# Attention, MoE and FFN in one kernel: GpSimd's weight chunk placed between the scatters of a pair's two tiles, for four pairs

## The chip, the cores and the metric

The kernel runs on one core of a Trainium2 chip. The metric is the device time of one execution in microseconds (us), as the median of several runs. Engines: PE (TensorE), DVE (VectorE), ACT (ScalarE), GpSimd (POOL in the profile) and SyncE (SP), which issues most transfers.

## What is computed

Three layers follow one another on 2304 tokens (4 sequences of 576) of 512 values:

```python
scores = scale * q @ k.T ; bias = slope[h] * -|i - j| ; mask = (0 <= i - j < 128)
x   = softmax(where(mask, scores + bias, -1e9)) @ v            # 8 heads of 64
...
noisy = x @ w_gate + log1p(exp(x @ w_noise)) * noise           # 8 experts, top 2 of each token
x   = sum over the two experts e: weight * (relu(x @ w1[e]) @ w2[e])
...
out = (relu(x @ w_in) ** 2) @ w_out                            # 512 -> 2048 -> 512
```

## The kernel before

Tokens are taken in 18 tiles of 128 rows. The attention stage is one loop over `v` from -2 to 38 (L553): an even `v` is the first four heads of tile `v // 2`, an odd one the other four. A turn of the loop issues three products of three neighbouring steps: the scores of step `v + 2` (`s_step`, matmuls at L257), the transposes of the probabilities of step `v + 1` (`t_step`, L279) and probabilities times values of step `v` (`pv_step`, L303). The score matmuls are small, 64 rows by 64 to 192 columns, so PE runs through many instructions in a microsecond here. Later stages use matmuls of 256 to 512 columns.

Tiles are gated in pairs: pair `p` is tiles `2p` and `2p + 1`, nine pairs from 0 to 8. What a pair needs is hung into the loop by a table written out by hand (L514 to L545, `at(v, slot, step)`): two transposed copies (`gate_t`, L333, L337), the gate product (`gate_w`, L344), the noise part (`gate_m`, L352), top 2 and ranks on DVE (`gate_o`, `rank`, `place`). `place` ends with `pos` (L422), which says for both tiles of the pair to which slot each token goes. Then `scatter(i)` (L425) writes the token numbers of tile `i` into the table `slots` in DRAM, for the first and the second expert of each token: two indirect transfers of 128 numbers, issued by GpSimd, each behind a `memset` of one element called `spacer` (L427, L428). For pair `p` the first tile's scatters are hung at turn `4p + 7`, the second's at turn `4p + 8`, but `pos` for both exists at the first; GpSimd works in order, and finds all four ready one behind the other.

Three times (`early_table`, L500, behind pairs 2, 4 and 6) a part of `slots` is read back and GpSimd gathers a tile of rows for the first expert (`gather`, L438), which PE transposes at L448.

Beside this the loop prepares the first seven of 64 weight chunks. A chunk is 128x1024 numbers; `prep_one` (L97) has GpSimd write a rounded copy (cast, L108) and the remainder (subtract, L110). The raw chunk is loaded by SyncE into one of two buffers (`load_to`, L88); `prep_one(i)` makes sure that chunk `i` is loaded and, when done, asks for chunk `i + 1`. The loop calls it at turns 2, 10, 14, 18, 22, 26 and 30 (L573); as GpSimd is ahead of the loop's code there, a chunk stands directly behind the four scatters of the pair before.

Of the kernel before, what the change touches and what calls it, by code (L numbers as in the profile page):

```python
# [49 lines left out]
def attn_moe_ffn(ctx: ExitStack, tc: tile.TileContext, qt, kt, vt, wgn, noise, w1, w2, w_in, w_out,  # L50
# [35 lines left out]
    nload, nprep = [0], [0]  # L86

    def load_to(n):  # L88
        while nload[0] < min(n, len(srcs)):
            i = nload[0]  # L90
            src, a = srcs[i]
            r = rawp.tile([128, 1024], F32, name="raw", tag="raw", bufs=2)
            nc.sync.dma_start(out=r if a is None else r.rearrange("p (a d) -> p a d", a=a), in_=src)
            raws[i] = r
            nload[0] += 1

    def prep_one(hi="act", lo="dve"):  # L97
        i = nprep[0]
        nprep[0] += 1
        load_to(i + 1)  # L100
        r = raws.pop(i)
        g, m = (i // 4) % 3, (i % 4) * 2048
        t = big["wb" if g else "wa"] if g < 2 else late["wc"]
        c = [t[:, m:m + 1024], big["wt"] if g == 1 and m == 6144 else t[:, m + 1024:m + 2048]]
        if hi == "act":
            nc.scalar.activation(out=c[0], in_=r, func=AF.Copy)
        else:
            nc.gpsimd.tensor_copy(c[0], r)  # L108
        eng = nc.vector if lo == "dve" else nc.gpsimd
        eng.tensor_tensor(out=c[1], in0=r, in1=c[0].bitcast(F32), op=OP.subtract)  # L110
        chunks[i] = c
        load_to(i + 2)


    width = {"wb": 7168, "wt": 1024, "xa": 3072, "wa": 8192, "ha": 6144, "xb": 3072, "hb": 4096, "tt": 1152, "wc": 8192, "ex": 3584, "et": 512}
# [36 lines left out]
    def load_q(i):  # L152
        Q[i] = qp.tile([128, 4, 128], F32, name="q", tag="q", bufs=4)
        nc.sync.dma_start(out=Q[i], in_=qt[i])

    def load_k(b, k0=0, k1=S):
        if b:
            K[b] = qp.tile([128, 4, S], F32, name="k", tag="k", bufs=2)
        nc.sync.dma_start(out=K[b][:, :, k0:k1], in_=kt[b][:, :, k0:k1])

    def load_v(n):
        b, p = divmod(n, 5)
        V[n] = qp.tile([128, 2, 8, 65], F32, name="v", tag="v", bufs=5)
        nc.sync.dma_start(out=V[n], in_=vt[b][:, 2 * p:2 * p + 2])
# [62 lines left out]
    def run(v, slot):  # L227
        for f, a in todo.pop((v, slot), []):
            f(*a)
# [42 lines left out]
    def t_step(v):  # L272
        PT[v] = []
        for j, p2 in enumerate(P2.pop(v)):
            flat = p2.rearrange("p a n -> p (a n)")
            ps = bank("a")[:, :384]
            for m in range(3):
                sl = slice(m * 128, (m + 1) * 128)
                nc.tensor.transpose(ps[:, sl], flat[:, sl], ident)  # L279
            pt = wk.tile([128, 3, 128], F32, name="pt", tag="pt", bufs=4)  # L280
            nc.scalar.activation(out=pt, in_=ps.rearrange("p (m c) -> p m c", m=3), func=AF.Copy)
            PT[v].append(pt)

    def pv_step(v):
        i, g = divmod(v, 2)
        px = bank("b")[:, :, :130].rearrange("p a (j d) -> p a j d", j=2)
        PX[i, g] = px
        mms = []
        for part in range(2):
            for j, pt in enumerate(PT[v]):  # L290
                for x in range(2):
                    b, t = divmod(2 * i + x, TB)
                    sl = slice(64 * x, 64 * x + 64)
                    for a in range(2):
                        h = 4 * g + 2 * j + a
                        if part == 0:
                            if a or t:
                                mms.append((x, a, j, pt[:, 2 * a, sl], vs(b, t - 1 + a)[:, h, :]))
                        elif a == 0 or t > 1:
                            r = slice(64 * a, 64 * a + 64)  # L300
                            mms.append((x, a, j, pt[r, 1, sl], vs(b, t - 2 if a else t + 1)[r, h, :]))
        for n, (x, a, j, l, r) in enumerate(mms):
            nc.tensor.matmul(px[64 * x:64 * x + 64, a, j, :], l, r,  # L303
                             start=not any(m[:2] == (x, a) for m in mms[:n]),
                             stop=not any(m[:3] == (x, a, j) for m in mms[n + 1:]), skip_group_check=True)
        del PT[v]

    def norm(i, g, n):
        px = PX[i, g]
        if n == 0:  # L310
            if g == 0:
                XI[i] = rows.tile([128, DM], F32, name="xi", tag="r", bufs=6)
            G["rs", i, g] = wk.tile([128, 2, 2, 2, 1], F32, name="rs", tag="rs", bufs=3)
            nc.vector.tensor_scalar(G["rs", i, g][:, 0], px[:, :, :, 64:65], 1e-9, None, op0=OP.add)  # L314
        elif n == 1:
            rs = G["rs", i, g]
            nc.vector.reciprocal(rs[:, 1], rs[:, 0])
        else:
            rs = G.pop(("rs", i, g))
            nc.vector.tensor_tensor(  # L320
                out=XI[i][:, g * 256:(g + 1) * 256].rearrange("p (j a d) -> p j a d", j=2, a=2),
                in0=px.rearrange("p a j d -> p j a d")[:, :, :, 0:64],
                in1=rs[:, 1].rearrange("p a j d -> p j a d").to_broadcast([128, 2, 2, 64]), op=OP.mult)
            del PX[i, g]
            if g:
                nc.sync.dma_start(out=xd[i * 128:(i + 1) * 128, :], in_=XI[i])
# [188 lines left out]
    for p in range(NT // 2):  # L515
        v = 4 * p + 3
# [30 lines left out]
    def v_free(n):  # L547
        b, m = divmod(n, 5)
        return 9 * b + min(2 * m + 3, 8)

    nq, nk, nv = 4, 1, 5
    load_to(1)
    for v in range(-2, NV + 3):  # L553
        s_step(v + 2, v)
        if 0 <= v + 1 < NV:
            t_step(v + 1)
        run(v, 4)
        if 0 <= v < NV:
            i, g = divmod(v, 2)
            pv_step(v)  # L560
            for n in range(3):
                norm(i, g, n)
            if g:
                if nq < NT:
                    load_q(nq)
                    nq += 1
                while nv < 5 * B and v_free(nv - 5) <= 2 * i + 1:
                    load_v(nv)
                    nv += 1
                if nk < B and 2 * i + 1 >= 9 * (nk - 1) + 1:  # L570
                    load_k(nk)
                    nk += 1
            if v % 4 == 2 and v != 6 and nprep[0] < 7:  # L573
                prep_one("pool", "pool")
        run(v, 5)

# [119 lines left out]
    def side_work(e, f):  # L696
        if f % 2 == 1 and nprep[0] < 8 * e + 12 and (e, f) != (E - 1, 7):
            prep_one()
        if e:
            next(decode, None)  # L700
        if e and e + 1 < E and f >= 3:
            gather(e + 1, f - 3)
# [244 lines left out]
    for f in range(3, 8):  # L947
        mm1_a(0, f)
        out_a(0, f)
        if f == 3:  # L950
            prep_one()
        if f == 4:
            weights()
        if f == 5:
            counts()
# [265 lines left out]
    for n, (s, u, kk) in enumerate(batches):  # L1221
# [8 lines left out]
        for k in range(2):  # L1230
            st, en = kk + k == 0, kk == 3 and k == 1
            for m, (p, o, lead) in enumerate(((P1, b13[:, 0:256], True), (P2, b26[:, 0:256], True),
# [9 lines left out]
                if m == 0:  # L1242
                    p1, u3 = tmp[2 + late_][:, 0:256], tmp[late_][:, 0:256]
                    x, y = [rows.tile([128, DM], F32, name="x", tag="r", bufs=6) for _ in range(2)]
                    i = s * SB + u * 128
# [70 lines left out]
```

## Time and profile before

| | us |
|---|---|
| median of 3 timed runs | 1002.08 |
| lowest and highest of them | 998.53, 1005.37 |
| the profiled execution's own time | 993.0 |
| its span, first to last instruction | 991.2 |
| PE busy in the span | 966.9 (98%) |
| DVE busy | 666.6 (67%) |
| ACT busy | 466.7 (47%) |
| GpSimd busy | 397.8 (40%) |

PE's mean granted clock is 0.995 of full speed. The profile is of one execution, so its durations add up to its own 991.2 us and not to the median. A row of a timeline gives the start, the length, engine, line, operation, output and input, and in square brackets the idle time of the engine before it and what ended that; "issue" there means that nothing which the profile shows was waited for. Matmuls overlap, so the time from one group's start to the next one's says more than the length of either.

### The profile page before, as it was taken

The numbers are of one execution on the slowest core, as the hardware profiler recorded it, in microseconds if no ns is written. First come the engines' busy times: TensorE is split into PE (matmuls) and PEld (weight loads), VectorE is DVE, ScalarE is ACT, GpSimd is POOL, SyncE is SP. The second block draws the span as 40 slices with busy tenths as digits, with TensorE's granted clock in tenths as the row PEclk, the third lists the DMA queues.
The fourth block names the chain that finished last, engine by engine and source line by source line (L and its number), as shares of the span: only waits on it lengthen the run. The fifth ranks groups of instructions, "written<-read, shape, count | busy, mean of one in ns | idle before, by whom it ended". The sixth has DMA issues, their size and how long they took to land. (4 is left out here: it accounts for less than half of the span.)

```text
span 991.2 us, 19643 instructions
## 1 busy us (share of the span) xinstructions
PE 966.9 (98%) x7438; PEld 883.3 (89%) x7438; DVE 666.6 (67%) x1453; ACT 466.7 (47%) x888; POOL 397.8 (40%) x431
## 2 busy tenths in 40 slices
PE   8989889999999999999999999999999999999997
PEld 6666668889898998989899888999999999999997
DVE  5656665456868585766667336678577899777773
ACT  7666762434433443433333336565545665433331
POOL 1354533214324162333326013633202524888880
PEclk9999999999999999999999999999999999999999
DMA  9656622555667576576654645684736884444331
GB/s 322 242 189 217 200 85 81 166 181 175 228 197 243 179 230 204 185 236 198 222 197 165 197 122 174 222 243 130 209 101 183 250 249 158 129 144 133 129 107 43
DMA packets 118199, 180.00 MB, mean 182 GB/s; under 512 B 11232, under 2 KB 66288, under 8 KB 117712
## 3 DMA queue, kind: packets, MB, share of 16 engines
q1 hardware_dynamic: 107120, 146.77, 45.8%
q0 software_dynamic: 10976, 31.90, 10.6%
q8 instruction: 59, 0.97, 0.4%
q14 instruction: 44, 0.36, 0.1%
HBM read 124.33 MB, written 54.30 MB: 180 GB/s over the span
## 5 line engine op out<-in xcount | busy, mean ns | idle before, releaser
L268 ACT ACTIVATE p<-p,mx 128x192 f32<-128x192 f32 x144 | 57.5, 448 | 39.3 <-DVE mx L262 37.8
L476 ACT ACTIVATE ha<-psa 128x384 fp32r<-128x384 f32 x64 | 31.3, 490 | 91.2 <-PE psa L472 88.6
L872 POOL TENSOR_TENSOR gs<-xb 128x256 f32<-128x256 f32 x62 | 59.1, 974 | 31.1 <-DVE wc L872 17.2
L689 POOL TENSOR_TENSOR et<-ex,et 128x512 f32<-128x512 f32 x16 | 20.9, 1304 | 113.3 <-DVE ex L685 113.3
L710 POOL DMA_INDIRECT yr<-yg,pos x36 | 37.0, 1029 | 72.3 <-DVE ha L477 45.2
L428 POOL DMA_INDIRECT slots<-tok,pos x36 | 35.1, 975 | 74.8 <-DVE rs L314 54.5
L477 DVE SCALAR_TENSOR_TENSOR ha<-psa,ha 128x384 fp32r<-128x384 f32 x64 | 35.4, 553 | 40.9 <-ACT ha L476 31.4
L262 DVE CUSTOM_DVE_ANT_0 p<-psb,bias 128x192 f32<-128x192 f32 x144 | 45.6, 351 | 13.0 <-PE psb L257 7.2
L472 PE MATMUL psa<-xa,wa 128*128 128x384 f32 x288 | 54.0, 337 | 0.2 <-DVE xa L450 0.2
L472 PE MATMUL psa<-xa,wc 128*128 128x384 f32 x288 | 53.3, 336 | 0.0
L791 PE MATMUL psb<-wa,ha 128*128 128x512 f32 x216 | 52.8, 396 | 0.0
L441 POOL DMA_INDIRECT xr<-xd,gidx x40 | 44.7, 1118 | 17.7 <-issue 6.8
L886 POOL DMA_DIRECT2D raw<-w x49 | 27.2, 558 | 60.8 <-DVE wb L872 18.4
L472 PEld LDWEIGHTS psa<-xa,wa 128*128 128x128 f32 x288 | 49.4, 188 | 1.2 <-DVE xa L450 0.5
L472 PEld LDWEIGHTS psa<-xa,wc 128*128 128x128 f32 x288 | 49.5, 188 | 0.2
L795 ACT ACTIVATE yo<-psb 128x512 f32<-128x512 f32 x38 | 22.7, 597 | 56.0 <-PE psb L791 43.1
L303 PEld LDWEIGHTS psb<-v,pt 64*64 64x64 f32 (+1 forms) x1056 | 34.3, 135 | 15.9 <-issue 12.3
L303 PE MATMUL psb<-v,pt 64*64 64x65 f32 (+1 forms) x1056 | 43.3, 231 | 4.2 <-issue 3.9
L791 PEld LDWEIGHTS psb<-wa,ha 128*128 128x128 f32 x216 | 39.5, 188 | 7.8
L791 PE MATMUL psb<-wb,ha 128*128 128x512 f32 x176 | 46.3, 397 | 0.0
L689 POOL TENSOR_TENSOR ex<-ex 128x512 f32<-128x512 f32 x12 | 15.6, 1304 | 74.3 <-DVE ex L685 74.3
L872 DVE TENSOR_TENSOR wc<-gs,wc 128x512 fp32r<-128x512 f32 x48 | 43.9, 953 | 0.0
(329 smaller groups left out, 2720.9 us busy)
## 6 DMA issues: line engine op xcount, KB each, us to landing
raw<-in_w_dram SPq DMA_DIRECT2D x64, 512.0 KB
xb<-gmid SPq DMA_DIRECT2D x72, 256.0 KB
v<-in_vt_dram SPq DMA_DIRECT2D x20, 520.0 KB
yg<-yo SPq DMA_DIRECT2D x40, 256.0 KB
raw<-w POOLq DMA_DIRECT2D x36, 256.0 KB
gmid<-yo SPq DMA_DIRECT2D x48, 192.0 KB
ex<-in_w_in_dram SPq DMA_DIRECT2D x16, 512.0 KB
ex<-in_w_out_dram SPq DMA_DIRECT2D x16, 512.0 KB
```

The lines of the kernel that those rows point to most:

```text
L262: nc.vector.tensor_tensor_reduce(out=p2[j][:, a, :], in0=ps[:, a, j, :], in1=bias[:, 4 * g + 2 * j + a, :], op0=OP.add, op1=OP.min, scale= ...
L268: nc.scalar.activation(out=p2[j][:, a, :], in_=p2[j][:, a, :], func=AF.Exp, bias=mx[j][:, a:a + 1], scale=-1.0)
L303: nc.tensor.matmul(px[64 * x:64 * x + 64, a, j, :], l, r, start=not any(m[:2] == (x, a) for m in mms[:n]), stop=not any(m[:3] == (x, a, j) ...
L428: st = nc.gpsimd.indirect_dma_start(out=slots, out_offset=bass.IndirectOffsetOnAxis(ap=pos[:, i, k:k + 1], axis=0), in_=tok[:, i:i + 1], i ...
L441: nc.gpsimd.indirect_dma_start(out=XR[e, j], out_offset=None, in_=xd[0:PARTS[j] * 128] if early else xd, in_offset=bass.IndirectOffsetOnAx ...
L472: nc.tensor.matmul(o, w[wp][:, f * 128:(f + 1) * 128], x[:, xp, d, :], start=(n == 0), stop=(n == 11))
L476: nc.scalar.activation(out=hi, in_=ps, func=AF.Relu)
L477: nc.vector.scalar_tensor_tensor(out=lo, in0=ps, scalar=0.0, in1=hi.bitcast(F32), op0=OP.max, op1=OP.subtract)
L689: nc.gpsimd.tensor_tensor(out=x, in0=af, in1=cf, op=OP.add)
L710: nc.gpsimd.indirect_dma_start(out=YR[i, k], out_offset=None, in_=yg, in_offset=bass.IndirectOffsetOnAxis(ap=pos[:, i, k:k + 1], axis=0))
L791: nc.tensor.matmul(py, h[:, hq], wc[wp][:, wsl], start=(f + n == 0), stop=(f == 7 and n == 2))
L872: f(**a)
```

## The change

`prep_one` gets a switch `more`: without it, it does not ask for the next chunk. A list `SPLIT` names the turns at which pairs 0, 1, 3 and 5 issue their first tile's scatters (7, 11, 19 and 27). At these turns the loop calls `prep_one` without the request, and three turns later `load_to` makes the request where it stood before. Turns 2, 18 and 26 stay as they were; 10, 14, 22 and 30 lose their chunk and keep the load.

```diff
-    def prep_one(hi="act", lo="dve"):
+    def prep_one(hi="act", lo="dve", more=True):
...
-        load_to(i + 2)
+        if more:
+            load_to(i + 2)
...
+    SPLIT = [4 * p + 7 for p in (0, 1, 3, 5)]
...
-            if v % 4 == 2 and v != 6 and nprep[0] < 7:
+            if v in SPLIT:
+                prep_one("pool", "pool", False)
+            elif v - 3 in SPLIT:
+                load_to(nprep[0] + 1)
+            elif v % 4 == 2 and v != 6 and nprep[0] < 7:
                 prep_one("pool", "pool")
```

The order of GpSimd's instructions at pair 1 before the change: the four scatters (`slots`, each with its `spacer`), then chunk 2 (`raw_966` into `wa`).

```order
L427 MEMSET spacer_106 1x1
L428 DMA slots_75<-tok_112,pos_104 9728x1
L427 MEMSET spacer_106 1x1
L428 DMA slots_75<-tok_112,pos_104 9728x1
L427 MEMSET spacer_106 1x1
L428 DMA slots_75<-tok_112,pos_104 9728x1
L427 MEMSET spacer_106 1x1
L428 DMA slots_75<-tok_112,pos_104 9728x1
L108 CAST wa_83<-raw_966 128x1024
L110 TENSOR_TENSOR wa_83<-raw_966,wa_83 128x1024
```

The same place after the change (lines here are one further than before):

```order
L428 MEMSET spacer_106 1x1
L429 DMA slots_75<-tok_112,pos_104 9728x1
L428 MEMSET spacer_106 1x1
L429 DMA slots_75<-tok_112,pos_104 9728x1
L108 CAST wa_83<-raw_966 128x1024
L110 TENSOR_TENSOR wa_83<-raw_966,wa_83 128x1024
L428 MEMSET spacer_106 1x1
L429 DMA slots_75<-tok_112,pos_104 9728x1
L428 MEMSET spacer_106 1x1
L429 DMA slots_75<-tok_112,pos_104 9728x1
```

Chunk 2 has moved ahead of the second tile's two scatters; the same holds for chunk 1 at pair 0, chunk 4 at pair 3 and chunk 6 at pair 5. Chunks 0, 3 and 5 and the scatters of the other pairs stand as before.

SyncE's queue around the load of the same chunk before the change, between stores of attention rows (`xd`) and loads of the next tiles (`q`, `k`, `v`):

```order
L164 DMA v_894<-in_vt_dram 128x1040
L93 DMA raw_966<-in_w1_dram 128x1024
L326 DMA xd_74<-xi_959 128x512
L154 DMA q_1055<-in_qt_dram 128x512
L159 DMA k_1057<-in_kt_dram 128x2304
```

And after it:

```order
L165 DMA v_896<-in_vt_dram 128x1040
L93 DMA raw_966<-in_w1_dram 128x1024
L327 DMA xd_74<-xi_961 128x512
L155 DMA q_1055<-in_qt_dram 128x512
L160 DMA k_1057<-in_kt_dram 128x2304
```

Nothing has moved on SyncE: the load stands at the same place, and only the chunk's use has come forward.

## Rows read from the trace of the kernel before

**Rows 1.** Busy time by stage: attention, then the first two stretches of experts.

```profile
30.00:175.00 145.00, 130.78 (x1865) 100.22 (x1865) 85.89 (x519) 84.65 (x212) 63.32 (x88) 0.96 0.48 163
175.00:400.00 225.00, 224.76 (x1306) 203.43 (x1305) 149.09 (x208) 89.01 (x137) 71.99 (x58) 1.00 0.63 200
```

**Rows 2.** Waits of PE over the span: engine, tile, line, releaser, us, times, longest.

```profile
PE psb L257 <- issue: 4.7, 11, 0.9
PE psb L303 <- issue: 3.9, 10, 0.5
```

**Rows 3.** GpSimd in order of time around pair 1: start us, us, instruction, idle before.

```profile
49.61 0.99 POOL L428 DMA_INDIRECT slots<-tok,pos  x1 [7.66 <-DVE rs L314]
...
53.45 0.96 POOL L428 DMA_INDIRECT slots<-tok,pos  x1 [0.22 <-issue]
54.41 1.05 POOL L108 CAST wa<-raw 128x1024 fp32r<-128x1024 f32 x1
55.54 2.35 POOL L110 TENSOR_TENSOR wa<-raw,wa 128x1024 fp32r<-128x1024 f32 x1
```

**Rows 4.** PE in order of time around pair 1, same columns.

```profile
51.05 0.66 PE L333 MATMUL psc<-cst,xi 128*128 128x128 f32 x4
51.63 1.11 PE L303 MATMUL psb<-v,pt 128*64 128x65 f32 x28
53.15 0.31 PE L303 MATMUL psb<-v,pt 64*64 64x65 f32 x3 [0.40 <-issue]
...
55.30 1.53 PE L257 MATMUL psb<-k,q 64*64 64x192 f32 x14 [0.87 <-issue]
56.76 1.54 PE L279 MATMUL psa<-cst,p 128*128 128x128 f32 x6
...
59.07 1.13 PE L303 MATMUL psb<-v,pt 128*64 128x65 f32 x32
60.13 0.62 PE L352 MATMUL psc<-trs,gt 128*128 128x16 f32 x4
60.68 0.88 PE L257 MATMUL psb<-k,q 64*64 64x192 f32 x16
61.49 0.87 PE L279 MATMUL psa<-cst,p 128*128 128x128 f32 x6
```

**Rows 5.** Stretches at pair 1 after its stop, and at pair 6: busy time, clock, DMA.

```profile
55.30:59.00 3.70, 3.70 (x28) 2.25 (x27) 1.96 (x11) 1.63 (x5) 2.55 (x3) 0.54 0.50 207
...
138.00:141.00 3.00, 1.45 (x21) 0.86 (x18) 0.06 (x1) 1.41 (x4) 1.59 (x3) 0.96 0.04 6
```

**Rows 6.** PE around pairs 0, 3 and 5, two rows of each.

```profile
35.53 1.07 PE L303 MATMUL psb<-v,pt 128*64 128x65 f32 x24
...
39.74 0.88 PE L279 MATMUL psa<-cst,p 128*128 128x128 f32 x6
...
85.90 1.11 PE L303 MATMUL psb<-v,pt 128*64 128x65 f32 x26
...
91.85 1.40 PE L279 MATMUL psa<-cst,p 128*128 128x128 f32 x6
...
120.75 1.11 PE L303 MATMUL psb<-v,pt 128*64 128x65 f32 x26
...
125.21 0.88 PE L279 MATMUL psa<-cst,p 128*128 128x128 f32 x6
```

**Rows 7.** GpSimd at the last pair's four scatters.

```profile
164.01 0.96 POOL L428 DMA_INDIRECT slots<-tok,pos  x1 [7.30 <-DVE pos L422]
```

**Rows 8.** PE beside the last pair's four scatters.

```profile
161.67 6.49 PE L472 MATMUL psa<-xa,wa 128*128 128x384 f32 x36
```

**Rows 9.** DMA queues from 36.4 to 39.4 us: packets, MB, share of 16 engines.

```profile
q1 hardware_dynamic: 234, 0.68, 69.3%
q0 software_dynamic: 97, 0.00, 2.3%
```

## The prediction

> **What bounds the kernel now.** I read the stages first, then the waits of PE, then GpSimd and PE in order of time around one pair's scatters. From 175 us on PE is busy 224.76 of 225 us; in the attention stage it is busy 130.78 of 145 us [rows 1]. So PE sets the time, and time that it loses in attention is not won back later: the stages behind it have no idle PE time that could take it up. The two largest waits of PE in the whole span are at L257 (4.7 us in 11 pieces) and L303 (3.9 us in 10), both attention matmuls, and both are put down to "issue": nothing that the profile shows was missing [rows 2].
>
> The order of time says when they come. At pair 1 (pairs are counted from 0) GpSimd starts the first of four scatters at 49.61 and ends the fourth at 53.45 + 0.96 = 54.41; they stand (53.45 - 49.61) / 3 = 1.28 us apart, and the weight chunk (cast 1.05, subtract 2.35) follows [rows 3]. PE runs dense until 53.15 - 0.40 = 52.75, which is 3.14 us after the first scatter began. From there it gets a few matmuls at a time with 0.4 to 0.9 us between them, and runs freely again from 55.30, which is 0.89 us after the fourth scatter's end [rows 3, 4]. The reader is to see that the stop begins a fixed while into the burst and ends with it: the length of the burst decides. After the stop the transposes of L279 take 1.54 us where a clean step takes 0.87 [rows 4], and the granted clock from 55.3 to 59 us is 0.54, which is mostly the lower of the two levels (1.2 for 2.4 GHz) [rows 5]. Bulk transfers are not the reason: at pair 6 PE is busy 1.45 of 3.00 us while the DMA engines are 0.04 busy [rows 5]. And the last pair's burst, from 164.01 on [rows 7], stops nothing: 36 matmuls run through it in 6.49 us, 0.18 us each [rows 8], where attention's L257 issues 16 in 0.81 us. It is the demand for instructions during a burst that counts, as if PE lived for some 3 us on what it had ahead.
>
> **What each stop costs.** A clean step goes from the start of L303 to L352 in 60.13 - 59.07 = 1.06 us, and L257 takes 61.49 - 60.68 = 0.81 [rows 4]; so L279 should start 1.87 us after L303 does. Where four transposes of a gathered tile stand between, I add 0.58, what the four of L333 take (51.63 - 51.05) [rows 4].
> Pair 0: 35.53 + 1.87 = 37.40, actual 39.74: 2.34 lost. Pair 1: 51.63 + 1.87 = 53.50, actual 56.76: 3.26, and 1.54 - 0.87 = 0.67 at the lower clock: 3.93. Pair 3: 85.90 + 2.45 = 88.35, actual 91.85: 3.50, and 1.40 - 0.87 = 0.53: 4.03. Pair 5: 120.75 + 2.45 = 123.20, actual 125.21: 2.01 [rows 4, 6]. Together 12.31 us: this is what the four split pairs can give back at most.
>
> **The change, part by part.** *Split of the burst.* In the four pairs a burst of four becomes two of two with the chunk between. Two scatters last 1.28 + 0.99 = 2.27 us; if the hold ends 0.89 us later, that is 3.16 us after the first began, and PE ran out at 3.14 [rows 3, 4]. A first half should therefore cost about nothing. The second half begins 2.27 + 3.48 (from 54.41 to the subtract's end at 57.89) + 0.3 = some 6.0 us after the first, so PE has some 2.9 us of undisturbed time between. By the clean order PE is then inside L303 and has L352, L257, L279 and the next L303 before it; I count about 54 matmuls in 3.14 us there against 49 (11 + 6 + 4 + 28) before the stop of pair 1, 10% more, so it runs out about 0.3 us sooner. I charge 0.3 us for each second half and nothing for the first: 1.2 us. The bounds for a half lie far apart, as the trace has no burst of two: 0 (the last pair's four scatters stop nothing) to 2.4 (a whole stop, as pair 0's). I take the value near the lower end since length and start of the stop fit each other within 0.02 us.
> *The chunk.* Cast and subtract are the same instructions, 3.4 us, and run some 2.6 us earlier in the same gap of GpSimd, which idles 7.66 us before this burst [rows 3]. No DVE or ACT work is added or taken. Cost nothing; the cover is that idle time.
> *The second tile's scatters* come 3.5 us later. Who reads what they write? The early tables, and these are taken behind pairs 2, 4 and 6, none of which is split. Nothing.
> *The added wait.* The chunk now needs its raw tile 2.6 us sooner, and two scatters are queued behind it on GpSimd. SyncE's order of loads is unchanged. If the tile is late, two scatters are late with it, and nobody waits for them before pair 4's table: on the path 0.
>
> What weighs against all this: from 36.4 to 39.4 us, PE's stop at pair 0, the DMA queues that moved anything are SyncE's and GpSimd's own, and the queue that carries instructions is not among them [rows 9]; so no fetch of a block of instructions was under way while PE stood. The Trainium skill, Runtime: NRT & Kernel Launch, section Instruction fetch mechanics, says that a sequencer fetches whole blocks ahead over a queue of its own and that this is mostly hidden. By that rule PE is not short of instructions and the stop has another cause that the burst brings with it; the sum would then be that of the second rival below, near 0, against 11.1 by the rows' timing. I lean on the timing.
>
> Sum against the profiled execution (993.0 us, of which 991.2 is the span): 12.31 - 1.2 = 11.1 us less, 981.9. The three timed runs have their median at 1002.08, 9 us above the profiled one; taken off there it is 991.0.
>
> **The rivals.**
> *Second halves still stop.* If what PE has ahead is not full again after 2.9 us, the second half holds it for half a stop, 1.2 us, in four pairs: 12.31 - 4.8 = 7.5 us gained, 994.6. For it: no row shows how fast the reserve fills. Against: after 55.30 PE goes at full demand at once [rows 4].
> *The hold goes by scatters, not by bursts.* Each of the four holds PE for 2.4 / 4 = 0.6 us, some 3 us late, split or not. Then only the lower clock behind pairs 1 and 3 goes (1.2 us), 1000.9. For it: no fetch in the stop [rows 9]. Against: the stop's end lies so near the burst's end.
> *The stop is in profiled executions only*, and the change does not do in a timed run what it says: 1002. For it: "issue" has no releaser. Against: the profiled execution is shorter than every timed one, not longer.
> *Slower.* If the stop belongs to the beginning of a burst, whatever its length, eight halves cost 8 x 2.4 = 19.2 us in place of 12.3: 6.9 more, 1009; with the lower clock behind each half (0.67 us, as behind pair 1) 1014. It is slower from 12.31 / 8 = 1.5 us a half on. For it: the constant 3.14 us at the start. Against: the last pair's burst has a beginning too and stops nothing [rows 7, 8].
>
> **How the numbers follow.** Forecast 0.57, second halves 0.12, by scatters 0.19, profiled only 0.05, slower 0.07. A measurement of this kernel can tell about 1%, 10 us, from no change. Forecast 991.0 lies just beyond that bound, and its own range is 985 (everything gone, and the runs' 3 us) to 995 (second halves half a stop). For 8 in 10 the range goes up to 1000.5, over the partial rival and the near part of the one by scatters. Faster by over 1%: most of the forecast's share and of luck in the runs, 0.50; within 1%: 0.46; slower: 0.04, the part of that rival in which the clock falls too.
>
> **What would show it.** Right: at pairs 0, 1, 3 and 5 PE has no wait for "issue" beyond 0.3 us a half, PE's waits at L257 and L303 fall to about half, L279 behind them takes 0.87, GpSimd shows two, chunk, two, and pairs 2, 4 and 6 stop as before for 2.4 us. The attention stage ends 11 us sooner and everything behind it keeps its length. Wrong: stops of over 1 us behind a second half; or stops gone and the stage no shorter, because ACT or DVE is then what PE waits for; or lower clock behind pairs 2 and 4, where there was none.

## The result and the profile after

| | before | after |
|---|---|---|
| median of 6 runs, us | 1000.85 | 991.14 |
| lowest and highest, us | 998.53, 1005.37 | 989.74, 992.83 |
| profiled execution, us | 993.0 | 989.87 |
| its span, us | 991.2 | 988.1 |

The ratio is 0.9895, with a 95% interval from 0.9868 to 0.9923: the change makes the kernel 1% faster, some 9.7 us. The forecast was 991.0. The two profiled executions lie only 3.1 us apart, because the one of before was shorter than all six of its timed runs. So the number came out right, but the steps behind it have to be looked at one by one.

Busy time by stage after the change (us, then PE, weight load, DVE, ACT, GpSimd, clock, DMA share, GB/s), beside [rows 1]:

```profile
30.00:175.00 145.00, 131.42 (x1906) 102.48 (x1905) 88.33 (x525) 87.42 (x218) 67.59 (x93) 0.98 0.52 171
175.00:400.00 225.00, 224.78 (x1311) 204.65 (x1311) 151.90 (x213) 88.49 (x138) 69.30 (x56) 1.00 0.62 195
```

The first window has a fixed length, so the gain does not show in its busy share alone: more matmuls have moved into it (1906 for 1865).

The waits of PE over the span after the change (engine, tile, line, releaser, us, times, longest), beside [rows 2]:

```profile
PE psb L304 <- issue: 5.8, 10, 1.2
PE psc L388 <- DVE oh L376: 2.9, 6, 1.5
PE psb L732 <- DVE yr L723: 1.8, 1, 1.8
PE psc L334 <- DVE xi L321: 1.3, 2, 0.9
...
PE psb L258 <- issue: 0.6, 2, 0.5
```

The two waits for "issue" were 4.7 + 3.9 = 8.6 us and are 0.6 + 5.8 = 6.4. In their place PE waits for DVE at L388, L334 and L732 (lines in these functions are one further than before, later ones six).

GpSimd in order of time at pairs 0 and 1 after the change (start us, us, instruction, idle before), beside [rows 3]:

```profile
39.85 0.99 POOL L429 DMA_INDIRECT slots<-tok,pos  x1 [0.16 <-issue]
...
41.15 0.97 POOL L429 DMA_INDIRECT slots<-tok,pos  x1 [0.22 <-issue]
...
48.76 0.96 POOL L429 DMA_INDIRECT slots<-tok,pos  x1 [6.56 <-DVE pos L423]
...
50.02 0.96 POOL L429 DMA_INDIRECT slots<-tok,pos  x1 [0.21 <-issue]
50.99 1.04 POOL L108 CAST wa<-raw 128x1024 fp32r<-128x1024 f32 x1
52.12 2.36 POOL L110 TENSOR_TENSOR wa<-raw,wa 128x1024 fp32r<-128x1024 f32 x1
...
54.68 0.99 POOL L429 DMA_INDIRECT slots<-tok,pos  x1 [0.16 <-issue]
```

The order is two scatters, chunk, two scatters, as the diff says. Pair 1's first scatter now starts at 48.76 and not at 49.61.

PE at the same place, beside [rows 4], and one row of pair 3:

```profile
37.53 0.87 PE L280 MATMUL psa<-cst,p 128*128 128x128 f32 x6
38.34 0.64 PE L345 MATMUL psc<-xt,wg_sb 128*32 128x256 f32 x8
...
44.78 0.20 PE L388 MATMUL psc<-oh,tri 128*128 128x8 bf16 x2 [1.53 <-DVE oh L376]
...
46.03 1.54 PE L280 MATMUL psa<-cst,p 128*128 128x128 f32 x6
47.36 1.06 PE L334 MATMUL psc<-cst,xi 128*128 128x128 f32 x4
48.35 1.50 PE L304 MATMUL psb<-v,pt 128*64 128x65 f32 x23
...
52.49 0.44 PE L334 MATMUL psc<-cst,xi 128*128 128x128 f32 x2 [0.88 <-DVE xi L321]
...
57.49 0.29 PE L304 MATMUL psb<-v,pt 64*64 64x65 f32 x2 [0.28 <-issue]
...
93.40 0.20 PE L388 MATMUL psc<-oh,ones 128*128 128x8 bf16 x2 [0.55 <-issue]
```

Behind pair 0's first half (scatters at 33.80 and 35.16) PE runs dense, where it lost 2.34 us before. Behind pair 1's second half it stops for 0.28 us, and the longest such stop of a half is 0.55 us, at pair 3. New are 1.53 us in which it waits for DVE at pair 0, 0.88 us at pair 1, and behind the first of these the lower clock (L280 in 1.54 us for 0.87).

DVE there:

```profile
42.87 0.36 DVE L263 CUSTOM_DVE_ANT_0 p<-psb,bias 128x192 f32<-128x192 f32 x1 [1.96 <-PE psa L280]
...
51.60 0.16 DVE L315 TENSOR_SCALAR rs<-psb 128x4 f32<-128x4 f32 x1 [3.12 <-PE psa L280]
```

The scores which L263 reads come from matmuls between 40.45 and 41.33, so DVE could have gone on 1.5 us sooner: DVE stops behind scatters too. The trace of before shows the same at pair 0:

```profile
39.42 0.16 DVE L314 TENSOR_SCALAR rs<-psb 128x4 f32<-128x4 f32 x1 [3.38 <-remote]
```

L314 works on what L303 has just made, and that had ended at 35.53 + 1.07 = 36.60 [rows 6]; it starts 2.8 us later and 1.0 us behind the end of the burst. In the trace after, with half a burst there, it starts 0.1 us behind those matmuls.

### The profile page after: what moved, and what is told of

The parts are those of the page before. It is cut to its first block, busy times and chain, and to the rows that moved or that the text cites. A ratio compares the mean times of both kernels' runs of the same rounds, so it can differ in the third digit from the quotient of the medians.

```text
span 988.1 us, 19643 instructions
## 1 busy us (share of the span) xinstructions
PE 962.4 (97%) x7438; PEld 881.4 (89%) x7438; DVE 667.9 (68%) x1453; ACT 465.4 (47%) x888; POOL 397.9 (40%) x431
## 5 line engine op out<-in xcount | busy, mean ns | idle before, releaser
L263 DVE CUSTOM_DVE_ANT_0 p<-psb,bias 128x192 f32<-128x192 f32 x144 | 45.7, 351 | 11.6 <-PE psa L280 6.6
L304 PEld LDWEIGHTS psb<-v,pt 64*64 64x64 f32 (+1 forms) x1056 | 34.9, 138 | 17.4 <-issue 14.0
L304 PE MATMUL psb<-v,pt 64*64 64x65 f32 (+1 forms) x1056 | 44.0, 234 | 6.1 <-issue 5.8
L110 DVE TENSOR_TENSOR wa<-raw,wa 128x1024 fp32r<-128x1024 f32 x20 | 25.3, 1266 | 29.2 <-ACT wa L106 29.2
```

The costliest lines, as they stand in the source:

```text
L263: nc.vector.tensor_tensor_reduce(out=p2[j][:, a, :], in0=ps[:, a, j, :], in1=bias[:, 4 * g + 2 * j + a, :], op0=OP.add, op1=OP.min, scale= ...
L304: nc.tensor.matmul(px[64 * x:64 * x + 64, a, j, :], l, r, start=not any(m[:2] == (x, a) for m in mms[:n]), stop=not any(m[:3] == (x, a, j) ...
```

## The experiments

Chips have numbers in the results of the experiments. The first profile and the result above have none on record; "the prediction's chip" stands for both here, though it is not shown that they are one chip. The table gives all experiments; the kernel before ran beside each of them.

| chip | kernel | median us | ratio, 95% interval |
|---|---|---|---|
| 4 | before | 1001.96 (23 runs, 997.78 to 1008.54) | |
| 4 | before, as an experiment | 1001.95 | 1.0007 [0.9982, 1.0033] |
| 4 | gap without the chunk | 1003.15 | 1.0016 [0.9989, 1.0042] |
| 4 | three and one | 992.72 | 0.9903 [0.9865, 0.9941] |
| 4 | no scatters | 979.34 | 0.9782 [0.9743, 0.9821] |
| 3 | before | 971.52 (17 runs, 970.35 to 973.86) | |
| 3 | whole bursts, chunks left out | 975.48 | 1.0044 [1.0029, 1.0058] |
| 3 | gap, chunks left out | 975.77 | 1.0044 [1.0030, 1.0059] |
| 3 | six pairs split | 981.14 | 1.0101 [1.0086, 1.0115] |
| 3 | two, one, one | 971.35 | 1.0004 [0.9996, 1.0013] |
| 9 | before | 971.21 (13 runs, 970.50 to 975.86) | |
| 9 | after, as an experiment | 970.61 | 0.9992 [0.9981, 1.0003] |
| 5 | before | 971.32 (13 runs, 970.40 to 975.51) | |
| 5 | wide bursts | 983.25 | 1.0092 [1.0059, 1.0125] |
| 5 | two, one, one | 971.34 | 0.9994 [0.9978, 1.0010] |
| 9 | before, beside the next run | 971.97 (12 runs, 970.12 to 977.00) | |
| 9 | small stores beside the bursts | 972.04 | 0.9997 [0.9977, 1.0016] |

**Before once more, on chip 4.** No edit.

> The kernel before, unchanged, for a second profile: the one on which the prediction rests was 993.0 us, 8 us under the median of the timed runs. Theory (a burst of four scatters outlasts what PE has ahead): PE stops at pairs 0 to 6, each time 3.1 us after the first scatter began and until 0.9 us after the fourth ended; if this execution is nearer to 1001 us, the difference lies in the attention stage, in longer stops or in more stretches at the lower clock behind them (each about 1.5 us). Rival (the stops have nothing to do with the 8 us): attention has the same length as in the first profile, and the difference lies in the stages behind.

Its waits of PE over the span:

```profile
PE psb L303 <- issue: 5.3, 12, 0.5
PE psb L257 <- issue: 3.7, 6, 1.0
PE psb L726 <- DVE yr L717: 1.8, 1, 1.8
```

The stops are there again at every pair from 0 to 6, from 3.1 to 3.3 us after the first scatter until 0.8 to 1.0 us after the fourth. The lower clock has moved to other pairs: from 68 to 86 us the granted clock is 0.72 here (the eighth number).

```profile
68.00:86.00 18.00, 15.88 (x198) 11.68 (x196) 9.09 (x61) 9.39 (x25) 7.59 (x9) 0.72 0.55 180
```

The span is 5.6 us longer than the first profile's. Of that, 3.1 us have come by the first scatter of pair 7; so the theory, which put the difference into the attention stage, had about half of it. The wait for `yr` far behind the stage, 1.8 us where it was 0.3, has another 1.5 us.

**No scatters.** Those of pairs 0 to 6 are left out, so their part of the table keeps its zeros, and row 0 is gathered where the tokens' rows belong.

```diff
     def scatter(i):
+        if i < 14:
+            return
```

> The kernel before without the scatters of pairs 0 to 6 (tables stay zero there, so the experts gather wrong rows; the amount of work behind is the same). Theory: no stop of PE in attention at all; the seven stops and their stretches at the lower clock go, 18 to 26 us: 975 to 983. Rival (something else that falls into the same place of each period stops PE, such as the gate's steps or the loads): stops stay, 995 to 1003.

979.34, which is 22.6 us less than before; no wait for "issue" is left in the stage, whose longest row of PE's waits is now one for DVE:

```profile
PE psc L387 <- DVE oh L375: 2.8, 5, 1.3
```

The stops come with the scatters.

**Three and one.** In the four split pairs the second tile's first scatter stands ahead of the chunk too.

```diff
         at(o + 1, 3, scatter, 2 * p)
+        if p in (0, 1, 3, 5):
+            at(o + 1, 3, scatter, 2 * p + 1, (0,))
...
-            at(o + 2, 3, scatter, 2 * p + 1)
+            at(o + 2, 3, scatter, 2 * p + 1, (1,) if p in (0, 1, 3, 5) else (0, 1))
```

> The changed kernel with the chunk behind the third scatter of pairs 0, 1, 3 and 5 in place of the second. Theory (length of the burst): three scatters last 2 x 1.28 + 0.99 = 3.55 us, held until 4.44, PE runs out at 3.14: a stop of 1.3 us in each of the four pairs, and less behind the single one; 993 to 996 us. Rival (any gap inside the four scatters is enough, as it lets a queue drain): no stop, 989 to 992. Rival (each scatter holds PE by itself, wherever it stands): 1001.

GpSimd at pair 1, first and third scatter of the burst and the single one behind the chunk:

```profile
49.23 0.97 POOL L433 DMA_INDIRECT slots<-tok,pos  x1 [6.58 <-DVE rs L315]
...
51.77 0.96 POOL L433 DMA_INDIRECT slots<-tok,pos  x1 [0.21 <-issue]
...
56.42 0.99 POOL L433 DMA_INDIRECT slots<-tok,pos  x1 [0.16 <-issue]
```

PE there:

```profile
52.78 0.21 PE L304 MATMUL psb<-v,pt 64*64 64x65 f32 x1 [0.41 <-issue]
53.50 0.31 PE L304 MATMUL psb<-v,pt 64*64 64x65 f32 x3 [0.51 <-issue]
53.62 0.38 PE L258 MATMUL psb<-k,q 64*64 64x192 f32 x2
...
58.23 0.87 PE L280 MATMUL psa<-cst,p 128*128 128x128 f32 x6
```

The stop begins at 52.78 - 0.41 = 52.37, which is 3.14 us after the first scatter, as the prediction read it at pair 1, and PE runs without a gap from 53.50, which is 0.77 us after the third's end at 52.73, where the prediction read 0.89. In the four pairs it begins 3.13 to 3.34 us after the first scatter and ends 0.69 to 0.79 us after the third. Place and length of a stop go by the burst, and a single scatter stops nothing. The time is a little below the theory's 993 to 996 and a little above the first rival's range, so it does not decide between these two; the rows do, since each of the four pairs stops. Nor is the burst of three worse than the halves: the four pairs lose 6.3 us in this trace (from first scatter to first scatter, as in the table further down) and 6.8 with halves. The two were taken on different chips, so neither this nor the 1.6 us between the medians is resolved.

**Gap without the chunk.** In the four pairs the second tile's scatters come a turn later, held back by a copy of one element that waits for DVE's maximum; the chunk stays behind them.

```diff
-            nc.gpsimd.memset(spacer, 0.0)
+            if hold:
+                nc.gpsimd.tensor_copy(spacer, G["mx"][0:1, 1:2])
...
-            at(o + 2, 3, scatter, 2 * p + 1)
+            at(o + 2 + (p in (0, 1, 3, 5)), 3, scatter, 2 * p + 1, (0, 1), p in (0, 1, 3, 5))
```

> The kernel before, with the second tile's scatters of pairs 0, 1, 3 and 5 held back by a copy of one element that waits for DVE two turns later (about 6 us after the first scatter, as in the changed kernel); the chunk stays behind them. Theory (the length of an unbroken burst decides, whatever fills the gap): as the changed kernel, 988 to 994 us, no stop over 0.5 us behind the first halves. Rival (the chunk's earlier place is what gains): no gain, 999 to 1003.

1003.15: my theory's number was missed by over 9 us. GpSimd's subtract of the chunk there:

```profile
62.38 2.34 POOL L110 TENSOR_TENSOR wa<-raw,wa 128x1024 fp32r<-128x1024 f32 x1
```

And DVE beside it:

```profile
62.84 1.91 DVE L364 TENSOR_TENSOR gs<-gs,nz_sb 128x16 f32<-128x16 f32 x1
64.78 0.17 DVE L366 TENSOR_TENSOR gs<-gs,psc 128x16 f32<-128x16 f32 x1
```

PE's waits:

```profile
PE psc L388 <- DVE oh L376: 10.7, 7, 2.7
PE psb L304 <- issue: 3.5, 4, 1.1
PE psc L334 <- DVE xi L321: 3.2, 4, 1.7
```

The issue waits fall as they should: all that are left are at pairs 2, 4 and 6, so a gap without the chunk saves PE its stop as well. But the late chunk runs into the gate steps of the next pair: a DVE operation on 128x16 takes 1.91 us (0.17 in most pairs) and ends at 64.75, when the subtract ends at 64.72; its neighbour, which has one input in PSUM, takes 0.17. So where the chunk stands matters by itself, and the change uses it well: it makes the gap without becoming late. (The Trainium skill, SBUF — State Buffer, section Who interferes with whom, says that a DVE instruction with two SBUF inputs contends with a GpSimd instruction that reads SBUF; the trace agrees, 1.91 us against 0.17.)

**Bursts and gaps with the chunks left out, on chip 3.** To free the gap of this collision, chunks 1, 2, 4 and 6 are set to zero at the start and not computed; one kernel keeps whole bursts, the other has the held scatters.

```diff
+        if hi == "pool" and i in (1, 2, 4, 6):
+            chunks[i] = c
+            load_to(i + 2)
+            return
...
+    nc.gpsimd.memset(big["wa"][:, 2048:6144].bitcast(F32), 0.0)
```

> Control for the next run: the kernel before with GpSimd's work on chunks 1, 2, 4 and 6 left out (those weights are zeros, set once at the start; the loads stay), the four scatters of each pair in one burst. What it takes away is the chunk behind the burst. Theory (the burst stops PE, the chunk behind it is hidden): as before, 997 to 1004. Rival (the chunk behind the burst costs by itself, by its reads against DVE's gate steps): 990 to 995.

> The held second halves again (pairs 0, 1, 3 and 5, two turns later), now with the work on chunks 1, 2, 4 and 6 left out (zeros), so that nothing of a chunk can meet DVE's gate steps behind the second half. In the run with the chunk there, a gate step with two inputs in SBUF took 1.91 us for 0.17 and ended with the chunk's subtract. Theory (a gap of any filling saves PE's stop; the chunk at the wrong place gave it back): 989 to 994, and against the control 8 us or more. Rival (the gap does not help without the chunk; second halves hold up DVE by themselves): 999 to 1003, no gain on the control.

975.48 and 975.77: no difference, and both slower than before, because the zeros at the start delay PE once, by 4.7 and 5.0 us: beside them DVE takes 6.33 us for the bias at the start where it took 1.44. The experiment answered another question. On this chip the kernel before takes 971.52, and whole bursts of four stop nothing.

**Six pairs split, on chip 3.** `SPLIT` for pairs 0 to 5.

```diff
-    SPLIT = [4 * p + 7 for p in (0, 1, 3, 5)]
+    SPLIT = [4 * p + 7 for p in range(6)]
```

> The changed kernel with the chunk between the tiles of all of pairs 0 to 5 (chunks 3 and 5 too, at pairs 2 and 4, behind which an early table is read). Theory: the stops at pairs 2 and 4 go as well, 2 x 2.5 to 4 us: 983 to 987. Rival (the early table and the gather come 3.5 us later and SyncE's queue stands behind the table): 989 to 995.

981.14, 1.0% slower. The first row of PE's waits:

```profile
PE psa L449 <- DMA xr<-xd,gidx: 8.1, 4, 4.1
```

Pairs 2 and 4 feed an early table. Scatters that come later there delay table, gather and transposes, so their split costs 8.1 us of waits. The stops that it was to remove do not exist on this chip, so nothing pays for it; on a chip with stops it was not tried.

**After once more, on chip 9.** No edit.

> The changed kernel unchanged, once more, to see what the gain hangs on. My theory (the stop behind a burst of four is a property of the chip that the kernel lands on): on a chip where the kernel before takes about 1002 us this one takes about 991, ratio 0.987 to 0.992; on a chip where the kernel before takes about 971.5 us its bursts of four stop nothing, the change has nothing to give back, and the two agree within 0.3%. The rival (chunk 1, 2, 4 or 6 standing earlier is a gain by itself, stop or no stop) has it 0.5% or more faster on either chip. A second rival (the four second halves cost DVE time by themselves) has it 0.3 to 0.6% slower where there is no stop.

970.61, ratio 0.9992: the change is worth nothing here. Pair 2 is not split, so its whole burst can be compared between the two chips in one and the same kernel. On the chip of the prediction, PE around the burst from 65.50 to 70.30:

```profile
69.08 0.21 PE L304 MATMUL psb<-v,pt 64*64 64x65 f32 x1 [0.45 <-issue]
69.83 0.27 PE L304 MATMUL psb<-v,pt 64*64 64x65 f32 x2 [0.53 <-issue]
70.54 0.21 PE L304 MATMUL psb<-v,pt 64*64 64x65 f32 x1 [0.44 <-issue]
71.25 0.27 PE L304 MATMUL psb<-v,pt 64*64 64x65 f32 x1 [0.49 <-issue]
```

On chip 9, around the burst from 60.95 to 65.75, first GpSimd:

```profile
60.95 0.97 POOL L429 DMA_INDIRECT slots<-tok,pos  x1 [5.38 <-DVE rs L315]
...
64.78 0.97 POOL L429 DMA_INDIRECT slots<-tok,pos  x1 [0.21 <-issue]
```

And PE:

```profile
64.53 0.87 PE L280 MATMUL psa<-cst,p 128*128 128x128 f32 x6
65.33 0.64 PE L345 MATMUL psc<-xt,wg_sb 128*32 128x256 f32 x8
65.90 1.13 PE L304 MATMUL psb<-v,pt 128*64 128x65 f32 x32
```

The scatters stand 1.28 us apart on both, with the same lengths, and PE runs through on one and stops on the other. So the stop goes with the chip (or with its state, or with how it is recorded, see below), and takes a burst and a dense stream of instructions to show.

**Wide bursts, on chip 5.** Before, with 128x1024 unused numbers set to zero ahead of each scatter.

```diff
-            nc.gpsimd.memset(spacer, 0.0)
+            nc.gpsimd.memset(big["ha"][:, 0:1024].bitcast(F32) if i < 14 else spacer, 0.0)
```

> The kernel before with one thing changed: ahead of each scatter of tiles 0 to 13 GpSimd sets 128x1024 unused numbers to zero instead of one, which puts some 1 us more between two scatters (about 2.3 us from one to the next where it was 1.28). The burst of four gets longer, from 4.8 to some 8 us. If the stop goes by the burst's length (PE stands from 3.14 us after the first scatter to 0.89 us after the last) and the kernel before takes about 1002 us, each stop grows by some 3 us in seven pairs: 1015 to 1022. If it goes by how densely the scatters stand (PE recovers what it lacks between two of them), the stops are gone: 980 to 990, as with the scatters left out. On a chip where the kernel before takes about 971.5 us there is no stop to change, and both theories have 971 to 973.

983.25. Chip 5 has no stops (before: 971.32 there), so length against density stays untried, and both theories missed the 12 us. PE's waits in the stage:

```profile
PE psc L387 <- DVE oh L375: 10.8, 6, 2.1
```

It is the late chunk again: 10.8 us, where the gap kernel had 10.7, and here with no stop beside it. At pair 1 the subtract runs from 57.08 to 59.43, and the gate step beside it, on which `oh` waits in turn, takes 1.80 us:

```profile
57.66 1.80 DVE L363 TENSOR_TENSOR gs<-gs,nz_sb 128x16 f32<-128x16 f32 x1
```

Pair 6 has a wide burst too but no chunk behind it, and it goes on to pair 7 in 12.54 us, as on chip 9 without wide bursts. So the late chunk costs the time here, not the wide burst. That explains most of the gap kernel's miss: what the gap gave there, the late chunk took. It is not all of it, as DVE stops behind the held halves as well (at pair 1 L315 waits 2.91 us), and a gap without any chunk was not tried on a chip with stops.

**Two, one, one, on chips 3 and 5.** Two scatters, cast, one, subtract, one.

```diff
+        if mid is not None:
+            scatter(mid, (0,))
         eng = nc.vector if lo == "dve" else nc.gpsimd
```

> The changed kernel with the third scatter between the chunk's cast and its subtract, so the four pairs have two, cast, one, subtract, one. Theory (what stops PE or DVE is an unbroken run of scatters): the second half's small losses, 0.3 to 1.5 us a pair, go: 987 to 991. Rival (the cast, 1.05 us, is too short a gap, and the third scatter adds to the first two): stops of about 1 us before the subtract, 991 to 995.

> The changed kernel with the second tile's two scatters apart as well: in pairs 0, 1, 3 and 5 GpSimd does two scatters, the cast, one scatter, the subtract, one scatter. Where the kernel before takes about 1002 us: if what is left behind the second halves (0.5 us of PE at pairs 1 and 5, 0.9 to 1.5 us of waits for DVE at pairs 0 and 1) belongs to the two scatters standing together, this is 2 to 4 us faster than the change, 986 to 990; if it is the number of scatters that counts, the same 991 as the change. Where the kernel before takes about 971.5 us: 971 to 972 by both.

971.35 and 971.34, no difference to before, as expected without stops. Whether it is better than the change where there are stops stays open: both times it met a chip that has none.

**Small stores beside the bursts, on chip 9.**

```diff
     def scatter(i):
+        if i in (2, 6, 10):
+            for n in range(8):
+                m = 2 * i - 4 + n
+                nc.sync.dma_start(out=many[:, m:m + 1], in_=pos[:, i, 0:1])
```

> The kernel before with more small pieces in flight during three of the bursts: ahead of the scatters of pairs 1, 3 and 5 SyncE stores one column of pos (128 numbers of 4 bytes, one piece each) eight times to unused memory, while GpSimd's four scatters are as they were; pairs 0, 2, 4 and 6 are unchanged, for comparison in the same execution. Theory one: the stop belongs to the load that many small transfers with their events put on something the engines share, whichever queue they come from, and the chips differ in how much of it they stand. Then the stops of pairs 1, 3 and 5 begin sooner than 3.14 us after the first scatter and last 1 us or more longer where the kernel before takes about 1002 us (1004 to 1012), and where it takes about 971.5 us a stop of over 0.5 us may appear at these pairs alone (974 to 982). Theory two: it belongs to GpSimd's own scatters. Then all seven pairs look alike, 1001 to 1004 or 971 to 974.

972.04, all pairs alike, no stop. Eight times 128 more small pieces do not bring the stop to a chip that has none; on a chip that has it, this was not tried, so it does not decide between the two theories.

## Why the prediction was right, and where it was not

The number came out right, 991.14 for 991.0, and in part by luck. The clean period of each pair, which the prediction had to work out, can now be read from the change on chip 9: from one pair's first scatter to the next one's it takes 13.52, 13.66, 13.76, 14.35, 13.66, 14.28 and 12.54 us. (Whole bursts on chip 3, with the chunks left out, have the same within 0.06 us.) What is above that is the loss. Worked out from the first scatters in each trace:

| loss, us | pair 0 | 1 | 3 | 5 | these four | 2, 4 and 6 |
|---|---|---|---|---|---|---|
| forecast for before | 2.34 | 3.93 | 4.03 | 2.01 | 12.31 | |
| before | 2.57 | 4.35 | 3.96 | 2.01 | 12.89 | 9.70 |
| after | 1.44 | 3.08 | 1.02 | 1.24 | 6.78 | 9.65 |
| before, chip 4 | 2.61 | 2.81 | 3.84 | 2.30 | 11.56 | 13.38 |

- *What each stop costs*: right, 12.31 against 12.89 in the same trace. All seven pairs lose 22.6 us there; leaving the scatters out gained 22.6 us of median on chip 4.
- *When a stop begins and ends*, 3.14 and 0.89 us: right, and shown apart from the trace that it was read from: bursts of four on chip 4 begin to stop PE after 3.13 to 3.34 us and end 0.84 to 0.97 us behind, and the burst of three shortens the stop by one scatter. Whether it is length that counts, or how many scatters follow each other so closely, was not separated.
- *Halves, as far as PE's own stop goes*: right. First halves show no "issue" wait, second halves 0.28 us at pair 1, 0.55 at pair 3, 0.19 + 0.15 at pair 5 and none at pair 0: 1.17 us together, where 1.2 stood in the sum. The size is right; the working is not quite, since the longest of them begin 2.3 to 2.6 us after the half's first scatter and end 0.5 us behind its last, where it had 2.8 and 0.9.
- *"No DVE or ACT work is added", cost nothing*: this step failed. No work was added, but the sum counted PE's stop alone, and DVE stops behind half a burst as well: at pair 0 L263 waits 1.96 us where it waits 0.59 on chip 9, and PE then waits 1.53 us for `oh` in place of 0.22; at pair 1 PE waits 0.88 us for `xi` behind the first half. That is 1.31 + 0.88 = 2.2 us. Behind pair 0's wait the clock is the lower of its two levels for part of the time (0.63 granted from 45 to 49 us), which L280, L334 and L304 show with 1.54 for 0.88, 1.06 for 0.63 and 1.50 for 1.12: 1.5 us. With the 1.17 this makes 4.8 of the 6.78 us; the rest I could not give to single waits. So the term for the halves was 6.8 us and not 1.2, and the split gave back 6.1 us against the profile of before and not 11.1. The two readings that the DVE part rests on, L263 on chip 9 and the clock after the change (the eighth number):

```profile
41.40 0.36 DVE L263 CUSTOM_DVE_ANT_0 p<-psb,bias 128x192 f32<-128x192 f32 x1 [0.59 <-PE psb L258]
...
45.00:49.00 4.00, 3.97 (x45) 3.30 (x43) 3.21 (x24) 3.15 (x9) 0.24 (x1) 0.63 0.77 302
```

- *Everything behind it keeps its length*: failed. The gain in the stage is 6.1 us, in the span 3.1; of the 3.0 us lost behind it, PE's wait for `yr` at L732 is 1.80 us where it was 0.33, which is half. The same 1.8 us stand in the trace of before on chip 4 and in that without scatters, and not in that of the change on chip 9, so the change is not needed for it. What brings it, and where the other 1.5 us went, was not tried.
- *Pairs 2, 4 and 6 as before*: right in sum (9.65 for 9.70), but by chance: pair 4 loses 4.19 us for 2.87 (waits of 1.18 and 1.13 us, and the lower clock behind), pair 6 2.80 for 4.33.
- *The signs that it named*: mixed. GpSimd's order is as said, and in the four split pairs PE's "issue" waits fall from 5.7 to 1.2 us, none over 1 us. But those at L257 and L303 do not halve over the span (8.6 to 6.4 us), as the ones of pairs 2, 4 and 6 grow from 5.0 to 6.1; L280 behind pair 0 takes 1.54 us and not 0.87; the lower clock comes behind pair 4, which it had named as a sign of being wrong; and the stage gains 6 us, not 11.
- *Profile to median*: here the missing gain came back. I took the profiled execution of before, 993.0, as the run to subtract from and carried its distance of 9 us to the median unchanged. But it was a short run: before varies by 7 us from run to run, and the trace on chip 4 (998.54) loses 24.9 us in the stage where the first lost 22.6, with other pairs at the lower clock. The change runs within 3.1 us. Against the trace on chip 4 its span is 8.7 us shorter. The runs say what the distance was: over the 31 runs of before on chip 4 the mean granted clock is 0.979 to 0.993, with its median at 0.988, and the time follows it, some 7.7 us for each 0.01 (correlation -0.92); the first profile has 0.995, and the six runs of the change 0.992 to 0.997. By that slope, an estimate, 5 of the 9 us were time at the lower clock, which the traces show behind stops, and so not a fixed distance but something that the change takes away in part. So 991.0 met 991.14 by two errors against each other: a gain sized 5 us too large against one short execution, and a typical run of before that loses more than that one.
- *Rivals.* "Profiled executions only" fell in the form that it was priced in, as the timed runs gained 9.7 us; whether recording has a part is left to the last section. "Second halves still stop", priced at 7.5 us, is nearer to what the trace shows (6.1) than the forecast's 11.1, but by way of DVE and the clock, not of PE's own reserve. "By scatters" fell with the burst of three, whose single fourth scatter costs nothing. "Slower" fell: no beginning costs a whole stop. That the stop has another cause than a shortage of instructions, for which the fetch rule spoke, is not refuted; the timing it doubted held all the same. The argument from pair 0 holds for five of the seven stops of that trace: the queue that carries instructions moved one packet each in those of pairs 3 and 5 and none in the others, so a stop does not need a fetch.

## What to carry to other kernels

A wait that no releaser explains may belong to the chip that the run landed on: compare the same rows on another chip before tuning for it, since this change is worth 1% on one and nothing on another. Where such a stop goes by the burst, cutting the burst helps on the chips that have it and cost nothing measurable on chip 9, as long as what fills the gap does not become late and nobody waits for the part that comes later (with six pairs cut it cost 1% on chip 3). Look at every engine that runs beside the burst, and not only at the one that sets the time: here DVE's own stop took back more than PE's. Whoever adds time ahead of a GpSimd operation that reads SBUF should look which two-input DVE operations it will then run beside: here 1.91 us for 0.17, and 12 us of the whole kernel where six chunks came late.

## What was not expected of the hardware

Two kinds of chips: 1001 to 1002 us on the prediction's chip and on chip 4, 971 to 972 us on chips 3, 5 and 9, for one kernel. Of the 30 us between them, 22.6 go with the scatters of seven pairs; the other 8 are open.

The traces of the two kinds differ in another way. The issues of the four scatters of pair 2 in the trace after the change, on the prediction's chip:

```profile
slots<-tok,pos POOLq DMA_INDIRECT x4
```

And on chip 9, where the last column is the median time from issue to landing:

```profile
slots<-tok,pos POOLq DMA_INDIRECT x4, 2.4
```

On the prediction's chip the column is empty, since the trace lacks part of the landings: 8,941 such events are recorded there for 9,976 on chip 9, and in the first trace of before there is none from 3 us into a burst to the end of the stop, at pairs 1 to 6. At pair 0 they come as densely as on chip 9, and PE stops there all the same; chip 4 has both too. So where PE and DVE stop, the record mostly has holes as well. That fits a stop which comes with the recording of events itself, as it fits a path of that chip which both need; every run here was recorded, so none can tell them apart. Against recording alone speak pair 0, a stop without a hole, and the kernel without scatters, whose trace on chip 4 has holes and no stops (8,817 events; the 28 scatters left out make some 420 of the difference, an estimate from the 15 events that each of the 24 added stores brought on chip 9). What the stop is stays open.
